# Attention, then SiLU and squared-ReLU layers: three weight tiles split early and kept in DRAM as halves

## The chip, the cores and the metric

One core of one Trainium2 chip runs the whole program. The metric is the device time in microseconds (us); the medians below are over three runs.

## The reference, cut to what matters

```python
attn = softmax(scale * q @ k.T + bias, causal window of 128)     # 4 x 8 heads, 576 tokens, head size 64
x = (attn @ v) as [2304, 512]
h = x @ w_in1;  x = (h * sigmoid(h)) @ w_out1                    # 512 -> 2048 -> 512
h = relu(x @ w_in2);  out = (h * h) @ w_out2                     # 512 -> 2048 -> 512
```

Inputs and weights have more mantissa than TensorE's fp32r takes in one pass. So each operand is split into a high part (rounded to fp32r) and a low part (what is left), and each product is three matmuls: high x high, high x low, low x high.

## The kernel before, in words

All engines' instructions stand in the order in which the Python code emits them (a schedule written by hand), and SP issues nearly all transfers, in that order, on one queue. There are four stretches:

- the attention, interleaved with the first product of layer 1 (`mm1`, L491);
- the second product, `mm2` (L540): 72 slots n of 12 or 24 matmuls. For each, 256 KB of the activation come back from DRAM (`load_g`, five slots ahead), ACT makes the high part and DVE the low part (`split_g`, L530, called two slots ahead);
- the third, `mm3` (L606), 112 steps: layer 2's first product, by a seven-product (Strassen-like) scheme;
- the fourth, `seven` (L688), 72 steps of 21 matmuls, the same scheme for layer 2's second product. Steps 2d and 2d+1 share the operand pair d: `load_a` (L627) fetches it from DRAM as two transfers of 256 KB, `sums_a` makes the three sums per half on DVE (four instructions, L657 to L660), `hi_a` the high parts on ACT (L678, L679), `lo_a` the low parts on DVE (L685, L686). The first sixteen steps go over weight tiles 0 to 3 for two row blocks, then 4 to 7 for both; so tile 3 is first read at step 3, 4 at step 8, 5 at step 9, 6 at step 10, 7 at step 11.

Weights arrive as 64-bit words. A tile x = (layer, 0 for w_in or 1 for w_out, i) holds two chunks of 128 x 512 and passes through: `w_load` (1 MB in two transfers, L389); `w_first` (DVE, L399 and L400), `w_abs` (ACT, L407), `w_join` (DVE, L411), which make fp32 out of the words; `w_sums` (DVE, L440 to L444 for w_out), the sums of the seven-product scheme. `convert` (L775) schedules these. `w_put` (L448) then keeps the result in DRAM (1 MB), and later `w_get` (L455) fetches it back into one of two 8 KB places (`raw`, called `own`, or `g2`, called `in_g`), and `finish` (L785) splits it: `w_hi8` (ACT, L465) and `w_lo8` (DVE, L470), twice each, of 1024 and 768 columns. The parts stand in two buffers of the pool `wp`, which rotates through 16; they come free as `mm3` is done with layer 2's w_in tiles.

The order around the change is a table: `then(phase, n, what)` puts work behind slot or step n of the second, third or fourth stretch (phases 2, 3, 4), and `do(phase, n)` emits it there. Tiles (1, 1, 0) to (1, 1, 2) are converted in phase 2, (1, 1, 3) to (1, 1, 7) in phase 3 (L1003). The lines of L1012 to L1019 say when each is fetched and finished: for (1, 1, 3) to (1, 1, 7) between step 102 of phase 3 and step 8 of phase 4.

Of the kernel before, what the change touches and what calls it, by code (L numbers as in the profile page):

```python
# [8 lines left out]
F32 = mybir.dt.float32  # L9
F32R = mybir.dt.float32r  # L10
I32 = mybir.dt.int32
# [3 lines left out]
ALU = mybir.AluOpType  # L15

P = 128
WINDOW = 128
BLK = 512
# [6 lines left out]
def kernel(  # L26
# [21 lines left out]
    nc = tc.nc  # L48
    B, NHP, S, _ = v.shape
# [6 lines left out]
    wp = ctx.enter_context(tc.tile_pool(name="wp", bufs=NF))  # L56
    raw_p = ctx.enter_context(tc.tile_pool(name="raw", bufs=1))
    x_p = ctx.enter_context(tc.tile_pool(name="x", bufs=1))
# [2 lines left out]

    x2d = tc.dram_tile([P, KC, NT], F32, name="x2d")
    wd = tc.dram_tile([P, 2, NF // 2, 16 * P], F32, name="wd")
    gd = [tc.dram_tile([P, NF, NT], F32, name=f"g{layer}d") for layer in range(2)]


# [304 lines left out]
    w_t, raw_t = {}, {}  # L371
# [6 lines left out]
    def w_load(x, raw):  # L378
        layer, io, i = x
        raw_t[x] = raw.rearrange("p (a n t) -> p a n t", a=2, t=2)  # L380
        w = (w1, w2)[layer].bitcast(I32)
        if layer == 0:
            nc.sync.dma_start(
                out=raw_t[x].rearrange("p a n t -> p a (n t)"),
                in_=w[2 * i:2 * i + 2, io].rearrange("a p n -> p a n"),
            )
        else:
            for a in range(2):
                nc.sync.dma_start(  # L389
                    out=raw_t[x][:, a].rearrange("p n t -> p (n t)"), in_=w[i + NI * (1 - a), io]  # L390
                )

    def words(x):
        return raw_t[x][..., 0], raw_t[x][..., 1]
# [58 lines left out]
    def w_get(x, raw):  # L453
        raw_t[x] = raw.rearrange("p (a n t) -> p a n t", a=2, t=2)
        nc.sync.dma_start(out=raw.bitcast(F32), in_=wd[:, x[1], x[2]])  # L455

    def needed(x, t, w):
        n = slice(0, 8 * P) if t == 0 else slice(0, 6 * P) if x[1] else slice(2 * P, 8 * P)
        return w[:, n]
# [21 lines left out]
    NI = NF // 2  # L481
# [290 lines left out]
    def then(phase, n, what, *a):  # L772
        todo.setdefault((phase, n), []).append((what, a))
# [5 lines left out]
    def convert(phase, x, place, first, ahead=3):  # L779

        then(phase, first - ahead, lambda: w_load(x, place()))
        for j, stage_ in enumerate((w_first, w_abs, w_join, w_sums)):
            then(phase, first + j, stage_, x)

    def finish(x, *when):  # L785

        for (phase, n), (stage_, t) in zip(when, ((w_hi8, 0), (w_lo8, 0), (w_hi8, 1), (w_lo8, 1))):
            then(phase, n, stage_, x, t)
# [8 lines left out]
    with tc.manual_schedule():  # L797
# [5 lines left out]
        with tc.tile_pool(name="at", bufs=2) as ap, tc.tile_pool(  # L803
            name="ps", bufs=1, space=bass.MemoryType.PSUM
# [157 lines left out]
        with tc.tile_pool(name="gp", bufs=1) as gp_, tc.tile_pool(  # L962
            name="acc2", bufs=4, space=bass.MemoryType.PSUM
# [29 lines left out]
            for i in range(4):  # L993
                n = 4 + 10 * i
                convert(2, (1, 0, i), own, n)
                finish((1, 0, i), (2, n + 4), (2, n + 5), (2, n + 5), (2, n + 6))
            for x, place, n in (
# [2 lines left out]
            ):  # L1000
                convert(2, x, place, n)
                then(2, n + 4, w_put, x)
            for i in range(3, NI):  # L1003
                n = (17, 29, 42, 57, 70)[i - 3]
                convert(3, (1, 1, i), own, n, 5)
                then(3, n + 6, w_put, (1, 1, i))
            for x, place, get, *when in (
                ((1, 0, 4), own, (2, 60), (2, 66), (2, 67), (2, 67), (2, 68)),
                ((1, 0, 5), own, (2, 69), (3, 1), (3, 2), (3, 2), (3, 3)),
                ((1, 0, 6), in_g, (3, 0), (3, 5), (3, 6), (3, 6), (3, 7)),  # L1010
                ((1, 0, 7), own, (3, 4), (3, 9), (3, 10), (3, 10), (3, 11)),
                ((1, 1, 0), own, (3, 88), (3, 95), (3, 96), (3, 96), (3, 97)),  # L1012
                ((1, 1, 1), in_g, (3, 90), (3, 98), (3, 99), (3, 99), (3, 100)),
                ((1, 1, 2), own, (3, 99), (3, 104), (3, 105), (3, 105), (3, 106)),
                ((1, 1, 3), in_g, (3, 102), (3, 107), (3, 108), (3, 108), (3, 109)),
                ((1, 1, 4), own, (3, 107), (3, 111), (4, 0), (4, 0), (4, 0)),
                ((1, 1, 5), in_g, (3, 110), (4, 1), (4, 1), (4, 2), (4, 2)),
                ((1, 1, 6), own, (4, 1), (4, 5), (4, 6), (4, 6), (4, 7)),
                ((1, 1, 7), in_g, (4, 3), (4, 8), (4, 8), (4, 8), (4, 8)),  # L1019
            ):  # L1020
                then(*get, lambda x=x, place=place: w_get(x, place()))
                finish(x, *when)

            then(2, 52, load_x2, room, 0)
            then(2, 57, early_sums)
# [188 lines left out]
```

## Time and profile before

| | |
|---|---|
| three runs | 889.6, 891.09, 893.23 us; median 891.09 |
| the profiled execution | 892.25 us, of which the span on the engines 890.5 us |
| busy in the span | PE 871.4 us (98%), DVE 599.1 (67%), ACT 459.2 (52%), POOL 138.2 (16%) |
| granted TensorE clock, mean | 0.994 of 2.4 GHz |
| second product | 321.7 to 518.8 us |
| third stretch | 518.8 to 698 us |
| fourth stretch | 698 us to the end |
| transfers | 170.51 MB, the 16 DMA engines busy 57.7% with SP's queue |

The view of stretches gives, for each, each engine's busy time, the granted clock (1.00 is 2.4 GHz, 0.50 is 1.2 GHz), the busy share of the DMA engines and what they moved. A timeline merges like instructions that follow each other and gives in brackets the idle time before them and what ended it. A transfer's time to landing runs from its issue on SP.

### The profile page before, as it was taken

Reading aid. Unit: us, or ns where it says so; the run is one execution under the profiler, and the core shown is the slowest. Engines: PE = TensorE matmul, PEld = TensorE weight load, DVE = VectorE, ACT = ScalarE, POOL = GpSimd, SP = SyncE. Lnnn points to the kernel's source line nnn. Section 1 sums busy time; section 2 is a strip of 40 time slices with the busy share of each in tenths; the row PEclk is TensorE's granted clock in tenths of the full one; section 3 lists DMA queues with packets and bytes.
Section 4 is the critical chain, followed back from the end, with each engine's and each line's share of the span. In section 5 each row is a group of like instructions: output and inputs, shape, how many; then the busy total and the mean of one; then the engine's idle time right before and its main releaser. Section 6 shows DMA issues by size and latency. Waiting matters only on the chain. (4 is left out here: it accounts for less than half of the span.)

```text
span 890.5 us, 17606 instructions
## 1 busy us (share of the span) xinstructions
PE 871.4 (98%) x6456; PEld 774.8 (87%) x6456; DVE 599.1 (67%) x1290; ACT 459.2 (52%) x991; POOL 138.2 (16%) x220
## 2 busy tenths in 40 slices
PE   6899999999999999999999999999999989999997
PEld 5577777777777998888888999999999979999997
DVE  6888765656563237767646547767667889999884
ACT  6777666666664224434333446656567643334331
POOL 5567544434432000000000000000000000000000
PEclk9999999999999999999999999999999999999999
DMA  9467566667552266677786345665667754444431
GB/s 262 133 210 251 172 196 195 183 192 217 150 166 96 95 225 214 223 248 272 254 278 219 119 176 206 246 251 200 253 212 262 249 194 131 150 131 140 142 101 44
DMA packets 113894, 170.51 MB, mean 191 GB/s; under 512 B 12176, under 2 KB 73616, under 8 KB 110736
## 3 DMA queue, kind: packets, MB, share of 16 engines
q1 hardware_dynamic: 113536, 169.25, 57.7%
q8 instruction: 51, 0.84, 0.4%
q14 instruction: 35, 0.29, 0.1%
q10 hardware_dynamic: 272, 0.13, 0.1%
HBM read 109.58 MB, written 59.77 MB: 190 GB/s over the span
## 5 line engine op out<-in xcount | busy, mean ns | idle before, releaser
L499 PE MATMUL h<-x,w 128*128 128x512 f32 (+1 forms) x960 | 207.7, 373 | 0.0
L552 PE MATMUL acc<-g,w 128*128 128x512 f32 (+1 forms) x960 | 197.3, 368 | 0.0
L499 PEld LDWEIGHTS h<-x,w 128*128 128x128 f32 x960 | 164.7, 189 | 37.4 <-issue 6.2
L552 PEld LDWEIGHTS acc<-g,w 128*128 128x128 f32 x960 | 167.3, 189 | 30.0
L704 PE MATMUL acc<-w,g 128*128 128x256 f32 x1512 | 184.5, 285 | 3.5 <-DVE g L685 2.7
L704 PEld LDWEIGHTS acc<-w,g 128*128 128x128 f32 x1512 | 183.3, 193 | 4.5 <-DVE g L685 3.1
L612 PE MATMUL a<-x,w 128*128 128x288 f32 x720 | 103.9, 295 | 0.0
L536 ACT CAST g<-l 128x512 fp32r<-128x512 f32 x72 | 44.8, 622 | 110.1 <-PE acc L552 101.2
L612 PEld LDWEIGHTS a<-x,w 128*128 128x128 f32 x720 | 98.7, 188 | 0.0
L512 DVE SCALAR_TENSOR_TENSOR t<-t,h 128x512 f32<-128x512 f32 x72 | 49.1, 684 | 67.5 <-ACT t L507 67.2
L537 DVE TENSOR_TENSOR g<-l,g 128x512 fp32r<-128x512 f32 x72 | 49.7, 691 | 66.6 <-ACT g L536 66.5
L304 POOL TENSOR_SCALAR z<-z,st 128x192 f32<-128x192 f32 (+2 forms) x120 | 64.8, 557 | 125.5 <-PE h L499 91.8
L507 ACT ACTIVATE t<-h 128x512 f32<-128x512 f32 x72 | 42.6, 594 | 63.9 <-PE h L499 63.6
L287 ACT ACTIVATE z<-z,st 128x192 f32<-128x192 f32 (+2 forms) x120 | 52.5, 439 | 17.9 <-DVE st L277 14.0
L678 ACT CAST g<-l 128x1024 fp32r<-128x1024 f32 x25 | 26.2, 1048 | 61.9 <-issue 25.2
L612 PE MATMUL d<-x,w 128*128 128x288 f32 x384 | 56.4, 295 | 0.0
L277 DVE CUSTOM_DVE_ANT_0 z<-so,bias 128x192 f32<-128x192 f32 (+3 forms) x136 | 39.0, 328 | 23.3 <-PE so L250 22.7
L612 PEld LDWEIGHTS d<-x,w 128*128 128x128 f32 x384 | 52.9, 188 | 0.0
L422 POOL TENSOR_TENSOR w<-spare,w 128x512 fp32r<-128x512 f32 x24 | 39.7, 1672 | 0.0
L685 DVE TENSOR_TENSOR g<-l,g 128x1024 fp32r<-128x1024 f32 x25 | 30.6, 1225 | 8.5 <-ACT g L678 8.5
L349 PEld LDWEIGHTS o<-pt,v 128*64 128x64 f32 x464 | 24.1, 135 | 12.9 <-issue 10.6
L349 PE MATMUL o<-pt,v 128*64 128x128 f32 (+1 forms) x464 | 32.6, 270 | 0.0
(134 smaller groups left out, 1066.9 us busy)
## 6 DMA issues: line engine op xcount, KB each, us to landing
g0d<-t SPq DMA_DIRECT2D x72, 256.0 KB, 2.8
l<-g0d SPq DMA_DIRECT2D x72, 256.0 KB, 3.9
raw<-in_w_dram SPq DMA_DIRECT2D x32, 512.0 KB, 5.0
g1d<-t SPq DMA_DIRECT2D x48, 288.0 KB, 2.5
l<-g1d SPq DMA_DIRECT2D x50, 256.0 KB, 3.3
spare<-in_w_dram SPq DMA_DIRECT2D x12, 1024.0 KB, 8.0
wd<-raw SPq DMA_DIRECT2D x12, 1024.0 KB, 4.5
raw<-wd SPq DMA_DIRECT2D x7, 1024.0 KB, 5.1
```

What stands on the lines that cost most here:

```text
L287: nc.scalar.activation(z[r, j, k], z[r, j, k], AF.Exp, bias=least[r, j:j + 1], scale=-1.0, accum_out=total[r, j:j + 1],)
L304: nc.gpsimd.tensor_scalar(z[r, j, k], z[r, j, k], share[r, j:j + 1], 1.0, ALU.mult, ALU.mult)
L349: nc.tensor.matmul(o[j * D:(j + 1) * D, :n], lhsT=vt[kb][:m, j * D:(j + 1) * D], rhs=pt[:m, j, kb, :n], start=kb == 0 or not m0, stop=kb == 1,
L422: nc.gpsimd.tensor_tensor(w[:, 1, a], words(x)[1][:, a].bitcast(F32), w[:, 0, a].bitcast(F32), ALU.subtract)
L499: nc.tensor.matmul(h[:, j * w:(j + 1) * w], lhsT=wi[:, wh, c * P:(c + 1) * P], rhs=x[:, xh, c, :w], start=c == 0 and i == 0, stop=c == KC ...
L507: nc.scalar.activation(t_t[n], h_t[n], AF.Tanh, scale=0.5)
L512: nc.vector.scalar_tensor_tensor(t, t, 1.0, h, ALU.add, ALU.mult)
L536: nc.scalar.copy(g[:, 0], t)
L537: nc.vector.tensor_tensor(g[:, 1], t, g[:, 0].bitcast(F32), ALU.subtract)
L552: nc.tensor.matmul(acc, lhsT=wo[:, a, c * P:(c + 1) * P], rhs=g[:, z, j * w:(j + 1) * w], start=f == 0 and i == 0, stop=f == NF - 1 and i ...
L612: nc.tensor.matmul(acc[to], lhsT=w[wh][:, c * P:(c + 1) * P], rhs=o[:, xh, c], start=r in (0, 1, 3) and c == 0 and k == 0, stop=c == 1 and ...
L704: nc.tensor.matmul(acc[to][:, half], lhsT=g[x][a], rhs=w[y][:, b], start=i == 0 and half == 0 and j == 0, stop=i == NI - 1 and j == 2, ski ...
```

## The change

Tiles (1, 1, 3), (1, 1, 4) and (1, 1, 5) are converted in phase 2, and split there too (`w_part`), inside the buffer `x`, which is free between the attention's output and `load_x2` of slot 52: two places for raw words, one each for the high and the low half. Each half (128 x 1792 words, 0.92 MB) goes to a new DRAM tile `hd`. They come back as halves, straight into two `wp` buffers (`w_get_parts`), behind steps 106 and 108 of phase 3 and step 0 of phase 4; ACT and DVE do nothing for them there. Tiles 6 and 7 are still converted in phase 3, at other steps, and are fetched behind steps 107 and 110 of phase 3 (before: 1 and 3 of phase 4).

```diff
+    hd = tc.dram_tile([P, 3, 2, 14 * P], F32, name="hd")
...
+    def w_part(x, t, h):
+
+        raw = words(x)[t].bitcast(F32).rearrange("p a n -> p (a n)")
+        hi, lo = (needed(x, t, w.rearrange("p (t n) -> p t n", t=2)[:, t]) for w in parts_t[x])
+        if h == 0:
+            nc.scalar.copy(hi, needed(x, t, raw))
+        else:
+            nc.vector.tensor_tensor(lo, needed(x, t, raw), hi.bitcast(F32), ALU.subtract)
+
+    def w_put_parts(x):
+        for h, w in enumerate(parts_t[x]):
+            nc.sync.dma_start(out=hd[:, x[2] - 3, h], in_=w[:, :14 * P].bitcast(F32))
+
+    def w_get_parts(x):
+        w_t[x] = [wp.tile([P, 2, 8 * P], F32R, tag="w", name="w") for _ in range(2)]
+        for h, w in enumerate(w_t[x]):
+            nc.sync.dma_start(
+                out=w.rearrange("p t n -> p (t n)")[:, :14 * P].bitcast(F32), in_=hd[:, x[2] - 3, h]
+            )
...
-            for i in range(3, NI):
-                n = (17, 29, 42, 57, 70)[i - 3]
+            room_x = x_p.tile([P, 16 * BLK], F32R, tag="x", name="w").rearrange("p (r n) -> p r n", r=4)
+            for j, x in enumerate(((1, 1, 3), (1, 1, 4), (1, 1, 5))):
+                n = 9 + 12 * j
+                parts_t[x] = [room_x[:, 2 + h] for h in range(2)]
+                convert(2, x, lambda j=j: room_x[:, j % 2].bitcast(I32), n)
+                for t, h in ((0, 0), (0, 1), (1, 0), (1, 1)):
+                    then(2, n + 4 + t + h, w_part, x, t, h)
+                then(2, n + 7, w_put_parts, x)
+            for i in range(6, NI):
+                n = (36, 57)[i - 6]
                 convert(3, (1, 1, i), own, n, 5)
                 then(3, n + 6, w_put, (1, 1, i))
...
-                ((1, 1, 3), in_g, (3, 102), (3, 107), (3, 108), (3, 108), (3, 109)),
-                ((1, 1, 4), own, (3, 107), (3, 111), (4, 0), (4, 0), (4, 0)),
-                ((1, 1, 5), in_g, (3, 110), (4, 1), (4, 1), (4, 2), (4, 2)),
-                ((1, 1, 6), own, (4, 1), (4, 5), (4, 6), (4, 6), (4, 7)),
-                ((1, 1, 7), in_g, (4, 3), (4, 8), (4, 8), (4, 8), (4, 8)),
+                ((1, 1, 6), own, (3, 107), (4, 3), (4, 4), (4, 4), (4, 5)),
+                ((1, 1, 7), in_g, (3, 110), (4, 6), (4, 6), (4, 7), (4, 7)),
...
+            for x, *get in (((1, 1, 3), 3, 106), ((1, 1, 4), 3, 108), ((1, 1, 5), 4, 0)):
+                then(*get, w_get_parts, x)
```

What the change makes of SP's order at the end of the third stretch and the start of the fourth. Before, from the tiles that `w_get` fetches behind steps 99 and 102 on (`g1d<-t` and `g1d<-g` are the third stretch's stores, `l<-g1d` and `g<-g1d` the halves of the operand pairs; the rows number lines of the kernel before):

```order
381 L455 DMA raw<-wd 128x2048
382 L455 DMA g_7373<-wd 128x2048
383 L1105 DMA g1d<-t 128x576 x3
384 L1105 DMA g1d<-g_5365 128x576
385 L641 DMA l<-g1d 128x2x256 x4
386 L455 DMA raw<-wd 128x2048
387 L641 DMA g_7494<-g1d 128x2x256 x2
388 L455 DMA g_7523<-wd 128x2048
```

With the change, from the stores of steps 104 to 106 on (`w<-hd` are the halves; L664 is L641 of before, L1136 is L1105):

```order
382 L1136 DMA g1d<-t 128x576 x3
383 L1136 DMA g1d<-g_5412 128x576
384 L476 DMA w<-hd 128x1792 x2
385 L456 DMA raw<-wd 128x2048
386 L476 DMA w<-hd 128x1792 x2
387 L456 DMA g_7387<-wd 128x2048
388 L1136 DMA g1d<-t 128x576 x3
389 L1136 DMA g1d<-g_5412 128x576
390 L476 DMA w<-hd 128x1792 x2
391 L664 DMA l<-g1d 128x2x256 x4
392 L664 DMA g_7498<-g1d 128x2x256 x2
```

Of row 385 before and 391 now, the first two transfers are pair d = 3. Between the stores of steps 104 to 106 (now rows 382 and 383; before, the rows just ahead of 381) and that pair stand now eight transfers of weights, where two stood (rows 381 and 382); the two of rows 386 and 388 of before have moved ahead of the pair.

SP's order in the second product, before, from the load of (1, 1, 0) on, behind slot 29 (`l<-g0d` are `load_g`'s):

```order
298 L448 DMA wd<-raw 128x2048
299 L527 DMA l<-g0d 128x512 x2
300 L389 DMA raw<-in_w_dram 128x1024 x2
301 L527 DMA l<-g0d 128x512 x2
302 L389 DMA raw<-in_w_dram 128x1024 x2
303 L527 DMA l<-g0d 128x512
304 L748 DMA x2d<-ev 128x512 x4
```

With the change:

```order
302 L449 DMA wd<-raw 128x2048
303 L550 DMA l<-g0d 128x512
304 L471 DMA hd<-w 128x1792 x2
305 L550 DMA l<-g0d 128x512
306 L390 DMA raw<-in_w_dram 128x1024 x2
307 L550 DMA l<-g0d 128x512
308 L390 DMA w<-in_w_dram 128x1024 x2
309 L550 DMA l<-g0d 128x512
310 L390 DMA raw<-in_w_dram 128x1024 x2
```

Two stores of halves (tile 4) and a third pair of loads (tile 5) stand now among the same five loads of activations.

DVE's order in the fourth stretch, with the change, from the sums of pair d = 3 on (L680 to L683 are L657 to L660 of before, L493 is L470, L708 and L709 are L685 and L686):

```order
968 L680 TENSOR_TENSOR s<-l 128x2x128
969 L681 TENSOR_TENSOR l<-l 128x2x128
970 L682 TENSOR_TENSOR s<-l 128x2x128
971 L683 TENSOR_TENSOR s<-l,s 128x2x128
972 L493 TENSOR_TENSOR w<-raw,w 128x1024
973 L708 TENSOR_TENSOR g<-l,g 128x2x512
974 L709 TENSOR_TENSOR g<-s,g 128x2x384
```

Between the sums and the low parts of d = 3 stands now the first split of tile 6; before, nothing stood there.

## Rows read from the trace of the kernel before

**Rows 1.** Stretches; in brackets the number of instructions.
```profile
core 0: us, PE busy (x) PEld busy (x) DVE busy (x) ACT busy (x) POOL busy (x), PEclk, DMA share, GB/s
321.70:518.80 197.10, 197.10 (x962) 167.14 (x961) 119.90 (x175) 74.38 (x109) 0.00 (x0) 1.00 0.66 227
518.80:698.00 179.20, 179.20 (x1346) 179.20 (x1346) 125.93 (x214) 111.87 (x232) 0.00 (x0) 1.00 0.64 232
728.00:738.00 10.00, 9.75 (x68) 9.55 (x68) 9.17 (x17) 3.84 (x5) 0.00 (x0) 0.83 0.40 121
738.00:886.00 148.00, 148.00 (x1234) 147.80 (x1232) 123.55 (x216) 52.70 (x64) 0.00 (x0) 1.00 0.38 121
```
**Rows 2.** PE's waits after 321.7 us: total, times, longest, us.
```profile
PE acc L704 <- DVE g L685: 2.7, 2, 2.1
PE acc L704 <- DVE g L686: 0.7, 3, 0.3
```
**Rows 3.** PE's timeline of the fourth stretch: start, us, what, idle before.
```profile
698.05 16.00 PE L704 MATMUL acc<-w,g 128*128 128x256 f32 x131
...
720.69 4.93 PE L704 MATMUL acc<-w,g 128*128 128x256 f32 x39 [0.25 <-DVE g L686]
727.74 0.62 PE L704 MATMUL acc<-w,g 128*128 128x256 f32 x3 [2.12 <-DVE g L685]
728.61 157.40 PE L704 MATMUL acc<-w,g 128*128 128x256 f32 x1297 [0.25 <-DVE g L686]
```
**Rows 4.** One stretch of 2 us behind the longest stop.
```profile
730.00:732.00 2.00, 2.00 (x12) 2.00 (x11) 1.75 (x3) 1.20 (x2) 0.00 (x0) 0.50 0.48 149
```
**Rows 5.** DVE's groups by form: what converts and splits a tile.
```profile
L399 DVE TENSOR_SCALAR raw<-raw 128x1024 int32<-128x1024 uint32 x20 | 17.2, 858 | 2.4 <-DMA raw<-in_w_dram 2.4
L400 DVE SCALAR_TENSOR_TENSOR raw<-raw 128x1024 int32<-128x1024 int32 x20 | 26.5, 1325 | 0.7
L411 DVE SCALAR_TENSOR_TENSOR raw<-raw 128x1024 int32<-128x1024 int32 x20 | 24.3, 1221 | 7.6 <-ACT raw L407 7.6
L440 DVE TENSOR_TENSOR raw<-raw 128x512 f32<-128x512 f32 x8 | 5.5, 686 | 0.0
L444 DVE TENSOR_TENSOR raw<-raw 128x256 f32<-128x256 f32 x8 | 3.4, 427 | 0.3
L470 DVE TENSOR_TENSOR w<-raw,w 128x1024 fp32r<-128x1024 f32 x11 | 13.4, 1221 | 8.8 <-ACT w L465 8.8
L470 DVE TENSOR_TENSOR w<-raw,w 128x768 fp32r<-128x768 f32 x11 | 10.5, 953 | 3.8 <-ACT w L465 3.8
```
**Rows 6.** Two fetches of 1 MB issued at 660.1 and 660.8 us.
```profile
L455 SPq DMA_DIRECT2D raw<-wd x1: 599/599/599, 660.1 to 660.1; - x1
L455 SPq DMA_DIRECT2D g<-wd x1: 376/376/376, 660.8 to 660.8; - x1
...
DMA to landing us min/median/max: 7.3/8.6/9.8
```
**Rows 7.** Four weight loads of 512 KB issued from 351.5 to 352.8 us.
```profile
L389 SPq DMA_DIRECT2D raw<-in_w_dram x4: 333/404/427, 351.5 to 352.8; - x4
...
DMA to landing us min/median/max: 4.3/5.9/7.2
```
**Rows 8.** Three stores of 288 KB, the last of step 106.
```profile
L1105 SPq DMA_DIRECT2D g1d<-t x2: 320/352/385, 689.7 to 690.1; - x2
L1105 SPq DMA_DIRECT2D g1d<-g x1: 399/399/399, 690.6 to 690.6; - x1
...
DMA to landing us min/median/max: 2.1/2.4/2.7
```
**Rows 9.** `load_a`'s two transfers on an empty queue, issued at 727.7 and 728.3.
```profile
DMA to landing us min/median/max: 3.0/3.1/3.3
```
**Rows 10.** The same for a pair issued at 709.0 and 709.6, behind 1 MB.
```profile
DMA to landing us min/median/max: 8.3/8.8/9.3
```
**Rows 11.** Pair d = 3: its first sum (DVE) and its first high part (ACT).
```profile
710.03 0.43 DVE L657 TENSOR_TENSOR s<-l 128x256 f32<-128x256 f32 x1
...
711.07 1.05 ACT L678 CAST g<-l 128x1024 fp32r<-128x1024 f32 x1 [4.22 <-DVE l L658]
```

More of the change, by code (lines that the diff above doesn't have):

```diff
@@ L455, in w_get @@
         nc.sync.dma_start(out=raw.bitcast(F32), in_=wd[:, x[1], x[2]])
+    parts_t = {}
+    def w_part(x, t, h):
[14 more added lines that the diff above has]
+            )
     def needed(x, t, w):
```

## The prediction

> **What bounds the kernel now.** I read the stretches first. In the second and the third, TensorE (PE) is busy from end to end, 197.10 of 197.10 us and 179.20 of 179.20 [rows 1]: no relief of another engine can shorten them, and extra work there costs something only if it makes PE wait. What can be won lies in the fourth. After 738 us it runs 1234 matmuls in 148.00 us [rows 1], 0.12 us each, so its 1512 need 181.4. It takes 188.0 us, from 698.05 to 886.01 (728.61 + 157.40) [rows 3]. **6.5 us are lost**, all before 738. The reader is to see two parts in the rows. PE's waits name DVE's low parts (L685, L686), 3.4 us in five stops, the longest 2.1 [rows 2]; each stop also costs a restart of some 0.25. And behind the longest stop (727.74 [rows 3]) the clock falls: 12 matmuls in 2 us at a granted 0.50, that is 1.2 GHz [rows 4], and 0.83 over ten us, 1.7 us lost [rows 1]. DVE is late there since it splits weight tiles between the operand pairs.
>
> **What the change takes away.** Three tiles' splits leave that place: each 1.22 + 0.95 = 2.17 us of DVE [rows 5]. If nothing new makes PE wait, all 6.5 us come back. That is the most that can be won.
>
> **What it adds in the second product.** Each of three tiles brings 0.86 + 1.33 + 1.22 + 0.69 + 2 x 0.43 = 4.96 us of conversion and 2.17 of splitting to DVE [rows 5], 21.4 us in all on top of 119.9 of 197.1 [rows 1]. It fits on average. By stretch: 72 slots in 197.1 us are 2.74 us each, of which `split_g` takes 0.69. That is the mean of L440, an instruction of the same 512 columns; 2.05 are left. The crowded place is slots 32 to 37, where tile 5 comes between (1, 1, 0) and (1, 0, 3): three `w_first` of 2.19, three `w_join` of 1.22, three sums of 1.55 to 1.7 make 15.0 us against six times 2.05 = 12.3, a backlog of 2.7. `split_g` runs two slots ahead; of those 5.5 us 2 x 0.69 go to the splits themselves, so 4.1 of lateness stay hidden, and DVE's work alone stops nothing. But DVE also waits for loads. In slots 27 to 31 stand a store of 1 MB (3.25 us: two 1 MB transfers land at 660.1 + 7.3 = 667.4 and 660.8 + 9.8 = 670.6 [rows 6]), two halves (2.45 to 2.8 each, below) and three tile loads of 2 x 1.4 (four pieces land between 355.8 and 360.0 [rows 7]). These are 16.6 to 17.3 us, with five activation loads some 20, in 13.7 us. The last load then comes about 3 us late, and 2.7 + 3 = 5.7 passes the 4.1 by 1.6. Lower bound 0 (the loads land in time), upper bound 2.7 (a whole slot). I take half of the 1.6: **+0.8 us**. SP's new stores wait for DVE's and ACT's parts, with the activation loads queued behind; these are five slots ahead (13.7 us), so that wait is hidden. What leaves the third stretch gains nothing, for PE never waits there. ACT's share moves along and is hidden by the same two slots.
>
> **What it adds ahead of the fourth stretch.** This is the main term. The last three stores of step 106 land at 691.8, 692.5 and 693.3 (690.6 + 2.7), 0.75 us apart [rows 8]. Transfers behind each other on SP's queue land one after the other: a pair of operand loads takes 3.0 and 3.3 us on an empty queue [rows 9], 8.3 and 9.3 behind 1 MB [rows 10]. So what SP issues before pair d = 3 must land before it: six halves, two tiles of 1 MB, four stores, and then the pair's two transfers. Per half, 0.92 MB: 2.8 us at the pace of 3.25 per MB [rows 6], 2.45 at that of the 512 KB loads [rows 7], 2.3 at that of the stores. I take the middle of the first two, since the halves' rows of 7 KB lie nearest to the 8 KB of the one and their DRAM layout is as new as the other's; 2.3 and 2.8 are the ends. Sum: 6 x 2.6 + 2 x 3.25 + 4 x 0.75 + 2 x 1.0 (the pair's pieces land 0.9 apart in [rows 9], 1.6 in [rows 10]; an empty queue is the simpler case, and I stay near it) = 27.1 us. Behind 693.3 that is **720.4 us** for d = 3, where its sums began at 710.0 before [rows 11].
>
> From there: from the first sum to the end of the first high part took 711.07 + 1.05 - 710.03 = 2.1 us [rows 11], so PE may begin at 722.5. It needs d = 3 at step 6, after 126 matmuls: 698.05 + 15.1 = 713.2. **It stands 9.3 us.** Then it waits for the low part: DVE now has a split of 1.22 before its own 1.22 [rows 5], ready some 4.0 us after landing, while PE is at its third matmul (2.1 + 0.24): 1.7, and 0.5 for L686. DVE, started late, owes the splits of tiles 6 and 7 as well before pair 4: its list from the landing (sums 1.7, first split 1.2, d = 3 2.0, sums 1.7, second split 0.9, a wait for ACT's high part of tile 7, estimated at 1.2, the length of the split that follows it, its split 1.2, then 1.2) ends at 11.1, PE's two steps at 2.1 + 2.2 + 5.0 = 9.3 plus two matmuls: another 1.5, and 0.4 for L686. Stops together 9.3 + 1.7 + 0.5 + 1.5 + 0.4 = 13.4. The clock falls behind the long stop as it does now [rows 4]: 1.7 if PE is what counts, nothing as far as PE would wait for pair 4 anyway; I take 0.9, ends 0 and 1.8. Against the 6.5 of now: 13.4 + 0.9 - 6.5 = **+7.8 us**.
>
> Sum on the profiled execution: 892.25 + 7.8 + 0.8 = 900.9. The median of the runs is 1.2 lower than that execution, so **899.7 us**, 1.0% slower. With the low ends (halves at 2.3, no clock, no stop in the second product) 899.7 - 1.8 - 0.9 - 0.8 = 896.2; with the high ones (+1.2, +0.9, +1.9) 903.7.
>
> A price by the skill, which the sum does without: the Trainium skill ("DMA: Bandwidth & Descriptors", Latency and other measured facts) says that a row pitch in HBM at large powers of two slows copies. The old tiles' rows lie 128 KB apart, the halves' 42 KB. By that the halves run at the quicker pace, and the estimate would be nearer to 897; no run here shows which of the two layouts is the slow one.
>
> **The rivals.**
> - *The queue doesn't hold the pair back* (faster). If a later transfer can pass an earlier one, or the halves are quick enough to land before 711, the old stops go and no new one comes: 891.1 - 6.5 + 0.8 = 885.4. For it: the splits do leave DVE at the one place where PE waits [rows 2]. Against it: the pairs that landed after 8.3 and 9.3 us [rows 10]. It decides if d = 3 lands by 711. The Trainium skill ("DMA: Bandwidth & Descriptors", Queues, rings and completion order) says that completion is not first-in, first-out for one issuing engine; by that rule this rival is likelier than I make it, but every pair in these rows landed in its order.
> - *The two stops balance* (no change). If the queue is drained by 717 or so, PE stands 5 to 6 us in place of 6.5, and the time stays within 887 to 895. It takes halves of about 2.0 us, quicker than any transfer in the rows per byte.
> - *DVE falls behind in the second product too* (much slower). If both crowded places, slots 14 to 20 and 32 to 39, miss by a whole slot of 2.74, and the clock falls once (1.7 [rows 1]): 899.7 - 0.8 + 5.5 + 1.7 = 906.1. For it: at slot 14 two `w_first` and a split stand in one slot, 2 x 2.19 + 1.22 = 5.6 us. Against it: the 4.1 us of cover.
>
> **How the numbers follow.** 0.5%, 4.5 us, is about what a measurement of this kernel can tell from no change: slower begins at 895.5, faster ends at 886.6. My case has 0.74, the first rival 0.08, the balance 0.11, the last 0.07. So slower 0.81, same 0.11, faster 0.08. The likeliest case's own range is 896 to 904. To hold 8 in 10 the range takes in about half of the balance below and the last rival's near end: 891 to 906. Predicted: 899.7.
>
> **What would show it right or wrong.** In the changed profile: PE's timeline of the fourth stretch with one stop of 7 to 11 us after 126 matmuls, released by ACT's L678 (its high part of d = 3); the pair's transfers landing 10 us or more after issue; a granted 0.50 behind the stop; no stop at 727; the second product between 197.1 and 199.8 us, with any waits of PE on DVE's L537 around its slots 35 to 40. I'm wrong if d = 3 lands before 711, if PE's stop is named for something else than that pair, or if the halves land less than 2.3 us apart.

## The result, and the profile after

The changed kernel takes a median of **900.64 us** (four runs, 897.76 to 901.63) against 890.35 (four runs) of the kernel before: a ratio of 1.0099, interval 1.0081 to 1.0118. It is 1% slower; forecast were 899.7 us and "slower" with 0.81. The profiled execution took 901.63 us (span 899.8, mean granted clock 0.987), 9.4 us above the 892.25 of before. The starts and ends of PE's four stretches say where these are:

| | before | after | difference |
|---|---|---|---|
| attention and first product, until PE begins the second | 321.72 | 323.62 | +1.9 |
| second product | 197.14 | 199.41 | +2.3 |
| third stretch | 179.19 | 179.19 | 0.0 |
| fourth stretch | 187.96 | 193.19 | +5.2 |

The stretches after, to be read against [rows 1] (the second line is the third stretch; then twice ten us around the long stop, and the rest):

```profile
core 0: us, PE busy (x) PEld busy (x) DVE busy (x) ACT busy (x) POOL busy (x), PEclk, DMA share, GB/s
323.60:523.00 199.40, 198.53 (x962) 166.79 (x961) 138.03 (x199) 82.74 (x118) 0.00 (x0) 1.00 0.75 268
523.00:702.20 179.20, 179.20 (x1346) 179.20 (x1345) 111.56 (x196) 107.40 (x227) 0.00 (x0) 1.00 0.55 195
718.00:728.00 10.00, 2.20 (x7) 1.75 (x8) 5.40 (x9) 2.57 (x3) 0.00 (x0) 0.60 0.59 202
728.00:738.00 10.00, 9.75 (x71) 9.37 (x70) 8.62 (x13) 5.40 (x6) 0.00 (x0) 0.88 0.32 105
738.00:895.40 157.40, 157.40 (x1312) 157.21 (x1311) 133.02 (x233) 56.33 (x69) 0.00 (x0) 1.00 0.39 121
```

DVE did 18 us more in the second product and 14 less in the third, as meant. PE's waits [rows 2] have changed their names: the longest is no longer for DVE's low parts but for ACT's high part (L701), and four small ones have come up in the second product (L575):

```profile
PE acc L727 <- ACT g L701: 7.1, 1, 7.1
PE acc L727 <- DVE g L708: 1.2, 1, 1.2
PE acc L575 <- DVE g L560: 0.9, 4, 0.2
PE acc L727 <- DVE g L709: 0.3, 1, 0.3
```

PE's timeline, of the second product and then of the fourth stretch (compare [rows 3]):

```profile
403.08 22.27 PE L575 MATMUL acc<-g,w 128*128 128x512 f32 x96 [0.16 <-DVE g L560]
425.57 3.02 PE L575 MATMUL acc<-g,w 128*128 128x512 f32 x12 [0.22 <-DVE g L560]
428.83 3.01 PE L575 MATMUL acc<-g,w 128*128 128x512 f32 x12 [0.24 <-DVE g L560]
432.09 91.10 PE L575 MATMUL acc<-g,w 128*128 128x512 f32 x491 [0.25 <-DVE g L560]
...
702.22 15.27 PE L727 MATMUL acc<-w,g 128*128 128x256 f32 x126
724.60 0.79 PE L727 MATMUL acc<-w,g 128*128 128x256 f32 x2 [7.11 <-ACT g L701]
726.60 7.64 PE L727 MATMUL acc<-w,g 128*128 128x256 f32 x45 [1.20 <-DVE g L708]
734.48 160.93 PE L727 MATMUL acc<-w,g 128*128 128x256 f32 x1339 [0.25 <-DVE g L709]
```

In the fourth stretch, where five stops stood before, the longest of 2.1 us [rows 2], there is now one long stop, after exactly the 126 matmuls that precede pair d = 3, and two short ones behind it. Who was late? ACT's L701 waited for DVE's sum L681, and DVE's first sum, L680, for a transfer (ACT's and DVE's timelines):

```profile
723.50 1.05 ACT L701 CAST g<-l 128x1024 fp32r<-128x1024 f32 x1 [15.13 <-DVE l L681]
...
722.47 0.42 DVE L680 TENSOR_TENSOR s<-l 128x256 f32<-128x256 f32 x1 [13.95 <-DMA l<-g1d]
```

That transfer is pair d = 3, issued at 709.5 and 713.5 and landed 12.0 and 8.8 us later, at 721.5 and 722.3 (before, the same pair was issued at 705.8 and 706.4 and took 3.3 and 3.5 us):

```profile
L664 SPq DMA_DIRECT2D l<-g1d x2: 524/524/524, 709.5 to 713.5; - x2
...
DMA to landing us min/median/max: 8.8/10.4/12.0
```

The DMA engines had no pause meanwhile (a share of 1.01 and 1.02 in the two stretches of ten us from 698 to 718), and behind the stop PE ran at a granted 0.50, 1.2 GHz:

```profile
698.00:708.00 10.00, 10.00 (x82) 10.00 (x82) 9.00 (x16) 6.90 (x12) 0.00 (x0) 1.00 1.01 421
708.00:718.00 10.00, 9.49 (x80) 9.29 (x78) 0.52 (x1) 0.38 (x1) 0.00 (x0) 1.00 1.02 391
...
726.00:728.00 2.00, 1.41 (x5) 0.50 0.02 7
728.00:730.00 2.00, 2.00 (x12) 0.50 0.76 254
730.00:732.00 2.00, 2.00 (x17) 0.92 0.01 2
```

### The profile page after: what moved, and what is told of

Same layout as the page of the kernel before. It is cut to its first block, busy times and chain, and to the rows that moved or that the text cites. A ratio compares the mean times of both kernels' runs of the same rounds, so it can differ in the third digit from the quotient of the medians.

```text
span 899.8 us, 17610 instructions
## 1 busy us (share of the span) xinstructions
PE 875.4 (97%) x6456; PEld 776.3 (86%) x6456; DVE 596.9 (66%) x1290; ACT 459.2 (51%) x991; POOL 138.1 (15%) x220
## 5 line engine op out<-in xcount | busy, mean ns | idle before, releaser
L575 PE MATMUL acc<-g,w 128*128 128x512 f32 (+1 forms) x960 | 198.7, 369 | 0.9 <-DVE g L560 0.9
L575 PEld LDWEIGHTS acc<-g,w 128*128 128x128 f32 x960 | 166.9, 189 | 32.6 <-DVE g L560 2.9
L701 ACT CAST g<-l 128x1024 fp32r<-128x1024 f32 x25 | 26.2, 1050 | 74.1 <-issue 32.9
L1167 DVE TENSOR_TENSOR ev<-a,ev 128x288 f32<-128x288 f32 x32 | 14.2, 455 | 36.4 <-PE a L635 36.4
L708 DVE TENSOR_TENSOR g<-l,g 128x1024 fp32r<-128x1024 f32 x25 | 30.6, 1223 | 8.3 <-ACT g L701 8.3
```

The lines of the kernel that those rows point to most:

```text
L575: nc.tensor.matmul(acc, lhsT=wo[:, a, c * P:(c + 1) * P], rhs=g[:, z, j * w:(j + 1) * w], start=f == 0 and i == 0, stop=f == NF - 1 and i ...
```

## The experiments

Theory **Q**: what SP issued before pair d = 3 must land before it; the halves and tiles now ahead of it make the stop. Rival **D**: DVE's order makes it (the split of tile 6 between the sums and the low parts of d = 3). For the second product, **L**: loads come late behind the stores of halves; rival **W**: DVE has more work there than slots. Totals of single runs move by 2 to 4 us with the start of the second product, where no kernel differs from another; so the stretches are compared. How far these scatter can be read from kernels with the same order there: the second product takes 199.24 to 199.63 us in the seven that leave it as the change made it, and the fourth stretch 193.01 to 193.92 us in four (after, put34, slots2846, pitch128); the third is 179.19 us in all eleven. Of the variants only reorder and last_two were run more than once:

| run | second product begins | second product | fourth stretch | run, us |
|---|---|---|---|---|
| before | 321.72 | 197.14 | 187.96 | 892.25 |
| after | 323.62 | 199.41 | 193.19 | 901.63 |
| five_behind | 320.98 | 199.56 | 189.00 | 894.93 |
| twice5 | 321.95 | 199.62 | 198.73 | 905.73 |
| split6 | 319.97 | 199.24 | 192.32 | 896.92 |
| reorder | 320.36 | 199.28 | 185.57 | 891.74 (median of 10) |
| put34 | 322.16 | 197.80 | 193.92 | 899.26 |
| slots2846 | 322.29 | 197.14 | 193.08 | 897.88 |
| pitch128 | 321.80 | 199.63 | 193.01 | 899.80 |
| pair_act | 322.39 | 199.56 | 189.66 | 897.01 |
| last_two | 321.23 | 197.14 | 182.62 | 886.13 (median of 6) |

**five_behind: two transfers behind the pair instead of ahead of it**

```diff
-            for x, *get in (((1, 1, 3), 3, 106), ((1, 1, 4), 3, 108), ((1, 1, 5), 4, 0)):
+            for x, *get in (((1, 1, 3), 3, 106), ((1, 1, 4), 3, 108), ((1, 1, 5), 4, 1)):
```

> One place in SP's order: the two fetches of tile 5's halves stand behind the operand pairs d = 3 and d = 4 in place of ahead of them; all other work, DVE's and ACT's order too, is that of the changed kernel. Theory Q (the queue holds pair d = 3 back: what SP issued before it must land before it): the pair lands two halves earlier, 2.17 + 2.31 = 4.5 us, so the stop behind 126 matmuls of the fourth stretch, 7.3 us in the changed kernel, becomes 2.8, with the follow-up stop of some 1.8 still there; the fourth stretch takes 188 to 189 us instead of 193.2, the profiled execution some 897. Rival D (DVE's order makes the stop, with tile 6's split between the sums and the low parts of d = 3): the stop stays at 7.3 and the fourth stretch at 193.

Measured: PE's timeline shows a stop of 2.64, the next of 1.49, and a fourth stretch of 189.00.

```profile
699.74 15.27 PE L727 MATMUL acc<-w,g 128*128 128x256 f32 x126
717.64 0.50 PE L727 MATMUL acc<-w,g 128*128 128x256 f32 x2 [2.64 <-ACT g L701]
719.64 169.10 PE L727 MATMUL acc<-w,g 128*128 128x256 f32 x1384 [1.49 <-DVE g L708]
```

The stop fell by 7.11 - 2.64 = 4.5 us, what two halves take. DVE's order is untouched, so D, which had the stop stay at 7.3, falls.

**twice5: two transfers more ahead of it**

```diff
                 then(*get, w_get_parts, x)
+                if x[2] == 5:
+                    then(*get, w_again, x)
```

(`w_again` issues the two fetches of `w_get_parts` once more, into the same buffers.)

> The two fetches of tile 5's halves are issued twice, the second time into the same buffers, so 1.84 MB more stand ahead of pair d = 3; nothing else differs from the changed kernel. Theory Q: the stop behind 126 matmuls grows by two halves, 4.4 to 4.6 us, from 7.3 to 11.8, and the fourth stretch from 193.2 to 197.7. Rival D: no change, 193. If the second fetch of the same place waits for the first to land, the pair comes later by some 2 us more, stop 13 to 14.

Measured: a stop of 12.57, between the two figures.

```profile
728.60 0.80 PE L733 MATMUL acc<-w,g 128*128 128x256 f32 x2 [12.57 <-ACT g L707]
730.59 168.90 PE L733 MATMUL acc<-w,g 128*128 128x256 f32 x1384 [1.19 <-DVE g L714]
```

The second fetch of a half was issued only as the first had landed (717.11 behind 717.05), which added about 1 us to the 4.4. Fewer and more bytes ahead of the pair move the stop both ways, by what they take: Q holds.

**split6: the split out of the way of d = 3's low parts, SP's order kept**

```diff
-                ((1, 1, 6), own, (3, 107), (4, 3), (4, 4), (4, 4), (4, 5)),
-                ((1, 1, 7), in_g, (3, 110), (4, 6), (4, 6), (4, 7), (4, 7)),
+                ((1, 1, 6), own, (3, 107), (4, 5), (4, 5), (4, 5), (4, 6)),
+                ((1, 1, 7), in_g, (3, 110), (4, 6), (4, 7), (4, 7), (4, 8)),
```

> SP's order is that of the changed kernel; tile 6 is split two steps later, so that DVE does the low parts of pair d = 3 right behind its sums, as in the kernel before; tile 7 is split one step later. Theory Q: the stop of 7.3 us behind 126 matmuls stays (the pair lands as late as ever, 19 to 21 us behind the start of the fourth stretch), only the second stop, 1.2 us with 0.8 of matmuls before it, shrinks to some 0.4 to 1.0; fourth stretch 191 to 193. Rival D: the stop of 7.3 goes to below 2, fourth stretch 186 to 188.

```profile
720.83 0.79 PE L727 MATMUL acc<-w,g 128*128 128x256 f32 x2 [7.15 <-ACT g L701]
722.08 37.77 PE L727 MATMUL acc<-w,g 128*128 128x256 f32 x297 [0.47 <-DVE g L708]
```

The long stop stays to a twentieth of a us, and the second falls from 1.20 to 0.47. So the split of tile 6 makes 0.7 us of the second stop, and nothing of the long one.

**reorder: tile 6 fetched earlier, tile 7 and tile 5's halves behind the pairs**

```diff
-                ((1, 1, 6), own, (3, 107), (4, 3), (4, 4), (4, 4), (4, 5)),
-                ((1, 1, 7), in_g, (3, 110), (4, 6), (4, 6), (4, 7), (4, 7)),
+                ((1, 1, 6), in_g, (3, 101), (4, 1), (4, 1), (4, 1), (4, 1)),
+                ((1, 1, 7), own, (4, 3), (4, 8), (4, 9), (4, 9), (4, 9)),
...
-            for x, *get in (((1, 1, 3), 3, 106), ((1, 1, 4), 3, 108), ((1, 1, 5), 4, 0)):
+            for x, *get in (((1, 1, 3), 3, 106), ((1, 1, 4), 3, 108), ((1, 1, 5), 4, 1)):
```

> The changed kernel with other places for the fetches alone: tile 6 is fetched behind step 101 of the third stretch (6 steps earlier) and split behind step 1 of the fourth; tile 7 behind step 3 of the fourth and split behind steps 8 and 9; tile 5's halves behind the pairs d = 3 and d = 4. So tile 7 (4.0 us) and two halves (4.5) no longer stand ahead of pair d = 3, and tile 6 (2.5) stands ahead of the halves of tile 3 where the queue still had room. Theory Q: pair d = 3 lands by 714 on the clock of the changed kernel's profile, PE needs it at 717.3, so no stop over 0.6 us behind 126 matmuls and no stretch at 1.2 GHz; the fourth stretch takes 182 to 185 us against 193.2, the whole 8 to 10.5 us less than the changed kernel, a median of 890 to 893: the relief of DVE that the change meant, with the second product's loss still paid. Rival (relief only moves the loss: DVE or the late fetches of tiles 5 and 7 stop PE further on, at steps 9 to 11): fourth stretch 187 or more.

Measured: no stop at d = 3 and no 1.2 GHz, a median of 891.74 us, 1.0002 of before (0.999 to 1.0013; before took 891.52 in the same set of runs): the whole loss of the change is gone, but no gain is left. The fourth stretch is 2.4 us shorter than before and the second product 2.1 longer. The fourth stretch took 185.57, half a us more than the upper end, for one stop came up further on:

```profile
714.99 12.44 PE L727 MATMUL acc<-w,g 128*128 128x256 f32 x101 [0.25 <-DVE g L709]
729.08 13.65 PE L727 MATMUL acc<-w,g 128*128 128x256 f32 x109 [1.65 <-DVE w L493]
```

L493 is here the split of tile 7, which PE needs at step 11, after 231 matmuls; its fetch, issued at 712.5 behind the halves, landed 10.8 us later, at 723.3. ACT's two high parts were done at 725.5, but DVE came to its split only at 726.9, since the low parts of one pair and the sums of the next (724.1 to 727.0) stood ahead of it. So the rival of this run was right in its kind, by the late fetch and by DVE's order, and small in size.

**put34: one store of halves six slots later (second product)**

```diff
-                then(2, n + 7, w_put_parts, x)
+                then(2, n + 7 + 6 * (j == 1), w_put_parts, x)
```

> In the second product the two stores of tile 4's halves are issued behind slot 34 in place of 28; nothing else differs from the changed kernel, DVE's and ACT's order included. In the changed kernel PE's matmuls stand apart at five places there: twice 79 to 82 us behind its start (slots 28 to 30) and three times 101 to 108 us behind it (slots 37 to 39), and the second product takes 199.4 us against 197.1 before. Theory L (the loads of the last crowded place come late behind those stores and DVE, without work to do, waits for them): the three stops at 101 to 108 vanish, DVE's waits on the loads of tile 5 and (1, 0, 3) fall from 0.7 to 1.4 each to below 0.4, the two at 79 to 82 stay, the second product takes 197.6 to 198.1. Rival W (DVE has more work there than slots): all five stay, 199.2 to 199.5. The fourth stretch is as in the changed kernel, some 193.

Measured: 197.80 us. The three stops of slots 37 to 39 are gone, with DVE's work unchanged; the two at slots 28 to 30 stay (0.15 us of idle time and less, so the view of waits names none). Of DVE's three waits for loads (w_first's first instruction, here L400) one is left, that for (1, 0, 3), of 1.1 us and not below 0.4 as expected; those ahead of it are gone. DVE's waits around these slots, in the changed kernel and then in this run:

```profile
DVE raw L400 <- DMA raw<-in_w_dram: 2.1, 2, 1.4
DVE w L400 <- DMA w<-in_w_dram: 0.7, 1, 0.7
...
DVE raw L400 <- DMA raw<-in_w_dram: 1.1, 1, 1.1
```

So at slots 37 to 39 it is L: DVE was not short of time but stood idle for loads, 1.4 + 0.75 + 0.77 us in the changed kernel, behind the stores.

**slots2846: tiles 4 and 5 at slots where nothing else is converted**

```diff
-                n = 9 + 12 * j
+                n = (9, 28, 46)[j]
```

> Tiles 4 and 5 are converted and split around slots 28 and 46 of the second product in place of 21 and 33, where no other tile is converted at the same slots; the same instructions, at other places, the fourth stretch untouched. If the second product's loss (2.2 us) comes from crowded slots alone, no stop is left there: 197.1 to 197.4 us, fourth stretch some 193. If the added 21 us of DVE work cost PE time wherever it stands, or if the store of tile 5's halves, now just ahead of the loads that slot 52 issues, holds these back, the second product stays above 198, or the third stretch begins with a stop.

PE's busy time of that second product:

```profile
322.30:519.40 197.10, 197.10 (x962) 1.00 0.76 271
```

197.14 us, as before the change. The conversion and the splits of three tiles are free in the second product if they stand at the right slots. The stops at slots 28 to 30 stood where tile 4's splits meet the work on (1, 0, 2) and (1, 0, 6); DVE has no idle time of over 0.3 us there in the changed kernel, from 397 to 411 us, so at those slots it is W.

**pitch128: the halves laid out in DRAM like the whole tiles**

```diff
-    hd = tc.dram_tile([P, 3, 2, 14 * P], F32, name="hd")
+    hd = tc.dram_tile([P, 16, 16 * P], F32, name="hd")
```

> The halves' DRAM tile gets rows 128 KB apart, as the whole tiles have, in place of 42 KB; the same bytes, orders and places otherwise. In the changed kernel halves land 2.2 us apart (0.92 MB, 2.4 per MB), whole tiles fetched between them 2.5 and 4.0 us behind the transfer before (1 MB). If the distance of the rows sets the pace: halves 2.8 to 3.4 us apart, pair d = 3 lands 4 to 7 us later, the stop behind 126 matmuls is 11 to 14 us and the fourth stretch 197 to 200 us; the stores of the halves slow down too. If not: 2.2 us apart, a stop of 7.0 to 7.4, fourth stretch 193.

Measured: the stop is 6.93 us, the halves of tile 5 land 2.26 us apart (2.31 in the changed kernel). The last line is that of these two:

```profile
722.82 0.80 PE L727 MATMUL acc<-w,g 128*128 128x256 f32 x2 [6.93 <-ACT g L701]
...
DMA to landing us min/median/max: 10.2/11.1/12.0
```

**pair_act: the pair on another queue**

```diff
-                nc.sync.dma_start(out=t[:, r], in_=gd[1][:, i + r::NI, c:c + 2 * P])
+                (nc.scalar if d == 3 else nc.sync).dma_start(out=t[:, r], in_=gd[1][:, i + r::NI, c:c + 2 * P])
```

> The two transfers of pair d = 3 are issued by ACT, on ACT's own queue, behind its activations of L1132, in place of SP's queue; SP's other transfers keep their order and their bytes. It parts two readings of 'what SP issued before must land before': the order of one queue, or the bytes that the DMA engines, busy at a share of 1.0 from 698 to 718 us, have been given already. Reading O (one queue's order): issued some 5 to 6 us behind the start of the fourth stretch, the pair lands 3 to 9 us later, ahead of halves that SP issued earlier; the stop behind 126 matmuls is 0 to 2 us instead of 7.3, and pair d = 4, still behind the halves on SP's queue, brings a stop of 2 to 5 us at step 8; fourth stretch 188 to 191. Reading B (the engines' bytes): the pair lands some 18 us or more behind the start of the stretch, as in the changed kernel less its neighbours at most, the stop is 5.5 to 7.5 us, fourth stretch 191 to 194.

Measured: the fourth stretch, 189.66, and the stop, 2.05, lie near O's figures, but not for O's reason. ACT issued the pair at 704.6 and 705.2, ahead of SP's halves of tile 5 (714.0), and it landed 9.4 and 10.9 us later, behind all that SP had issued by then, though that stood on the other queue. What it gained is what five_behind gained: two halves that no longer stood ahead. PE's stop:

```profile
718.46 0.51 PE L727 MATMUL acc<-w,g 128*128 128x256 f32 x2 [2.05 <-ACT g L701]
```

The edit did more than change the queue: SP waited 6.9 us, until ACT's first transfer had landed (713.98), before it issued the halves (714.04; the last section says why). What the pair would have done with the halves issued at 708 on SP's queue, as in the changed kernel, this run does not show. The view of the DMA queues (packets, MB, share of the engines' time; q1 is SP's, q10 ACT's) for 705 to 709 and 709 to 713 us:

```profile
q1 hardware_dynamic: 247, 1.61, 100.0%
q10 hardware_dynamic: 20, 0.02, 2.2%
...
q1 hardware_dynamic: 285, 0.95, 74.8%
q10 hardware_dynamic: 290, 0.28, 22.7%
```

First ACT's queue got next to nothing, then one packet for each of SP's. A second queue was no way around full engines here. Reading O missed the mechanism. B's, that the pair lands behind the bytes that the engines have been given before, fits; its times missed, since it counted halves that SP had not issued yet.

**last_two: a version built on the theory**

```diff
-            for j, x in enumerate(((1, 1, 3), (1, 1, 4), (1, 1, 5))):
-                n = 9 + 12 * j
+            for j, x in enumerate(((1, 1, 6), (1, 1, 7))):
+                n = (28, 46)[j]
...
-            for i in range(6, NI):
-                n = (36, 57)[i - 6]
+            for i, n in ((3, 17), (4, 29), (5, 42)):
...
-                ((1, 1, 6), own, (3, 107), (4, 3), (4, 4), (4, 4), (4, 5)),
-                ((1, 1, 7), in_g, (3, 110), (4, 6), (4, 6), (4, 7), (4, 7)),
+                ((1, 1, 3), in_g, (3, 102), (3, 107), (3, 108), (3, 108), (3, 109)),
+                ((1, 1, 4), own, (3, 107), (3, 111), (4, 0), (4, 0), (4, 0)),
+                ((1, 1, 5), in_g, (3, 110), (4, 1), (4, 1), (4, 2), (4, 2)),
...
-            for x, *get in (((1, 1, 3), 3, 106), ((1, 1, 4), 3, 108), ((1, 1, 5), 4, 0)):
+            for x, *get in (((1, 1, 6), 4, 3), ((1, 1, 7), 4, 5)):
```

> A version built on the theory: not tiles 3, 4 and 5 but the two last, 6 and 7, are kept as halves; they are converted around slots 28 and 46 of the second product and fetched behind steps 3 and 5 of the fourth stretch, behind the pairs d = 3, 4 and 5; tiles 3, 4 and 5 are converted in the third stretch, fetched and split as in the kernel before. So ahead of pair d = 3 stand two tiles of 1 MB, as before the change, and DVE has no weights to split behind step 2. Theory Q: pair d = 3 lands as in the kernel before, some 11 to 12 us behind the start of the fourth stretch, no stop is longer than 0.6 us, no 1.2 GHz, the fourth stretch takes 181.8 to 183.5 us (before 188.0); the second product 197.1 to 197.5. The whole: 4.5 to 6 us below the kernel before, 885.5 to 887. If the halves of 6 and 7, needed at steps 10 and 11, or the pairs behind them come late, a stop shows there and the fourth stretch takes 185 or more.

Measured: a median of **886.13 us, 0.9948 of before (0.993 to 0.9966; before took 891.11 in the same set of runs)**, faster than both kernels. The pair landed 3.2 and 3.4 us after its issue, and PE stops twice for a quarter of a us:

```profile
697.57 15.51 PE L727 MATMUL acc<-w,g 128*128 128x256 f32 x128
713.35 0.62 PE L727 MATMUL acc<-w,g 128*128 128x256 f32 x3 [0.27 <-DVE g L708]
714.21 165.98 PE L727 MATMUL acc<-w,g 128*128 128x256 f32 x1381 [0.25 <-DVE g L709]
```

The fourth stretch is 182.62 us, 1.2 above the 181.4 of its matmuls, and the second product 197.14. So the idea of the change, halves made in advance to spare DVE, is sound: 5.3 of the 6.5 us that were lost before can be had with it.

## Why the prediction was right, and where its sizes were off

**The verdict and the mechanism hold.** The long stop stands behind 126 matmuls and is released by ACT's L701 (L678 of before), as forecast; five_behind, twice5 and split6 show that it is the transfers ahead of pair d = 3. The rival that the queue doesn't hold the pair back falls with them. The Trainium skill ("DMA: Bandwidth & Descriptors", Queues, rings and completion order) says that completion isn't first-in, first-out; in the eleven profiles each of SP's 632 to 640 transfers landed behind the one that SP had issued before it, so here that rule changed nothing. The same section says that engines take turns between queues packet by packet, and pair_act agrees from 709 us on (285 and 290 packets), but not from 705 to 709 (247 and 20).

**The main term: 7.26 us of stop, not 9.3.** "Per half 2.6 us" was the step that was too large. From the last store of step 106 (landed 697.8) to the pair (722.3) went 24.5 us against 27.1 in the sum: six halves 13.6 in place of 15.6 (2.15 to 2.6 each, mostly 2.2), two tiles 6.5 (as forecast; 2.5 and 4.0), four stores 2.9 (3.0; part of their bytes moved within the 4.0, see the last section), the pair 1.5 (2.0). I had named halves under 2.3 apart as a sign that I'm wrong; they were, and the mechanism held all the same. The row pitch is not why they are quick, as pitch128 shows: with rows 128 KB apart they land just as close. So the price by the Trainium skill's rule on pitch ("DMA: Bandwidth & Descriptors", Latency and other measured facts) had the right pace for the halves, but this run speaks against the reason, at these distances. That page's figures begin at a pitch of 512 KiB, where it has 207 GB/s against 214 at a padded pitch; my prediction stretched them to 128 KB.

**The stops behind it.** The second, 1.7 forecast, took 724.60 to 726.60 less 0.24 = 1.76. The third, 1.5 + 0.4 for pair 4, did not come beyond 0.25: PE was at 1.2 GHz until about 730 and DVE got its list done meanwhile. What came in its place is the clock term: 45 matmuls from 726.60 to 734.48 took 7.88 where 45 x 0.12 = 5.4 and the stop 0.25 would be due, 2.2 us in place of 0.9 (bounds 0 and 1.8). The clock makes 1.9 of them (half of the 3.4 us at 0.50 until 730, then 0.08 of the 2 us at 0.92); the rest are restarts and short waits. I had taken half of it for hidden behind PE's wait for pair 4. Fourth stretch: +5.2 in place of +7.8.

**The second product: +2.3 in place of +0.8, inside the bounds of 0 to 2.7.** The place of slots 32 to 37 was found, its reason (loads late behind stores, put34) too; "I take half of the 1.6" was the wrong step, for it cost all of it. From one start to the next, 12 matmuls took 428.83 - 425.57 = 3.26 us where 12 x 79.30/349 = 2.73 are due: each stop costs 0.53, twice the 0.24 that the idle column shows, three of them 1.6. The rest, some 0.7, came at slots 28 to 30, which I had not looked at (slots2846 takes both away).

**What no step forecast.** +1.9 us came ahead of the second product, where nothing was changed. It began anywhere from 319.97 to 323.62 in the eleven profiles above, whose work up to there is the same: the scatter of the executions. A part of it goes with the granted clock: in four of them (after, twice5, put34, pair_act) PE was granted 1.2 GHz for 10.2 us ahead of the second product, in the other seven for 6.8, and the four begin it at 322.5 on the mean, the seven at 321.2. Why the clock differed stays open. Without the 1.9 the change cost 7.5 us in its profile, which lies within the interval of the medians (0.81% to 1.18%, 7.2 to 10.5 us), near its lower end. That the forecast of 8.6 came so near the 9.4 of the profiled execution is in part luck: the fourth stretch was taken 2.6 too high, the second product 1.5 too low, and the 1.9 came on top.

The rival of the balance was what reorder reached, 1.0002, by order and not by faster halves. The rival that DVE falls behind in the second product came true on a small scale and at another place: at slots 28 to 30, for some 0.7 us, while its slots 14 to 20 show no stop and at 37 to 39 DVE waited for loads.

## What to carry to other kernels

Before work is moved off a busy engine by storing and fetching its result, list what the queue must move ahead of the next operand that PE needs, in MB and in order: here 0.8 MB more per tile, and tiles ahead of an operand pair that had stood behind it, turned a possible gain of 5 us (last_two) into a loss. Fetch in the order of need, operands first, and choose for the longer way those pieces that are needed last. In a stretch where PE is full, added work on another engine cost nothing here or half a us per stop, depending on the slots of the work and of its transfers; look for slots with nothing else in them.

## What the runs showed of the hardware that I had not expected

- A small transfer on a second queue is not quick while the first keeps the engines busy: 2 x 256 KB on ACT's queue took 9.4 and 10.9 us, got 20 of 267 packets in their first four us, and then one for one. Why the first 4 us gave so little stays open.
- SP did not issue the second piece of pair d = 3 until tile 7 had landed (713.46 and 713.45), though they share no data, and so on for the next pieces, each with a landing just ahead of it. Eight transfers were then under way, and in none of the eleven profiles were there ever more. The trace shows why: the program gives its transfers eight semaphores of completion in turn, those on SP's queue and on ACT's together, and before it issues one it waits for the transfer eight before, which had the same semaphore; in none of the eleven profiles was a transfer issued before that one had landed. So this limit stands in the program's instructions; whether the chip has one of its own further up, no run shows. It cost nothing in the changed kernel, since the engines had work; in pair_act it held SP's halves back for 6.9 us. SP's longest wait from 709 to 717 us:

```profile
SPq L664 <- DMA g<-wd: 3.4, 1, 3.4
```

- Tiles 6 and 7, 1 MB each from the same DRAM tile, landed 2.5 and 4.0 us behind the transfer before them in the changed kernel, and 2.5 and 3.7 to 4.3 in the seven variants that fetch them in the same order. Landings in order do not mean that the engines finish one transfer before they begin the next: in the last 2.05 us before tile 7 landed (711.4 to 713.45) the queue moved 276 packets of 2304 bytes, 0.64 MB, which are rows of the four stores behind it, and two of these stores then landed 0.4 and 0.6 us behind the one before. In reorder, where no stores stand behind tile 7, it took 2.5.
